# Seven block products in place of eight for the first expert of the first block

## The chip, the cores and the metric

The kernel runs on one core of a Trainium2 chip, in one launch. The metric is the time of one execution in microseconds. Its engines are TensorE (PE in the profile; its weight loads PEld), VectorE (DVE), ScalarE (ACT), GpSimd (POOL) and SyncE (SP), which issues nearly all transfers. All arithmetic is fp32.

## The reference

Two stages follow each other. A state-space layer (mamba2_ssd) works on 4 sequences of 768 tokens, 8 heads of 32 channels and a state of 16; its result is laid out as 3072 tokens of 256 features. On that works a mixture of four experts with all experts active:

```python
# per head, with the decays' running sums inside each chunk
y = (C B^T * L) x + (C state) * decay          # L: products of decays, causal
# then, x: (3072, 256), w1: (4, 256, 1024), w2: (4, 1024, 256)
p = domain_probs / (domain_probs.sum(-1, keepdims=True) + 1e-09)
for e in range(E):
    h = np.maximum(x @ w1[e], 0.0)
    out += p[:, e:e + 1] * (h @ w2[e])
```

## The kernel before

**Tiles.** The 3072 tokens are 24 chunks of 128. Two chunks make a *pair* of 256 tokens. Five *blocks* of pairs follow each other: three of two pairs (scheme B in the code) and two of three pairs (scheme H). The 1024 hidden features of an expert are four *feature blocks* `fb` of 256, sixteen over the four experts; expert 0 has 0 to 3, expert 1 has 4 to 7. A *block product* multiplies a 256x256 weight block's half with 256 tokens: two matmuls of 128x256 into one PSUM bank (`product`, L864).

**Fewer products.** Two feature blocks and two pairs of tokens make a 2x2 by 2x2 product of blocks, for which scheme B takes seven products where plain multiplication takes eight. This needs sums of weight blocks (`operands`, L955; stored in DRAM once made, L960, and loaded by later blocks, L952), sums of token blocks (`token_sums`, L974) and sums of the results. Scheme H does the same with three by three. Products are numbered in the code: in the first layer of scheme B, products 1 and 2 need only the first pair of tokens and the plain weights of the first feature block of the two; 6, 7, 5 and 3 need sums of weights, and 6, 7, 5 and 4 sums of tokens.

**The first layer with seven (`twos_first`).** Products accumulate in one bank, and intermediate values of the bank are kept aside: `snap` (L873) copies a bank to SBUF on ScalarE, `seed` (L878) copies such a value back into a bank, `combine` (L891) adds two of them on VectorE or GpSimd, and `gated` (L899) applies ReLU and the expert's gate on VectorE, out of the bank. The order for two feature blocks is 1, snap, 6, snap, 2 on a seed, 7, snap, 4, gate, 5 on a seed, gate, 3, subtraction in the bank (L1026), gate.

**The second layer (`second`, `visit`).** The results go into accumulators of two products each (a *house*) that are taken up and put down: seeded into a bank, added to, copied out (L1124, L1127).

**The state-space stage.** For each chunk `decays` scans the running products of decays on VectorE (L489), `fade` makes a part of the output operand on GpSimd (L499), `mask` the C operand on ScalarE (L465); `scores` multiplies (L472) and masks by VectorE (L788); `outputs` (L505, with the state L810) gives the tokens of the chunk, copied to SBUF by ScalarE (L825). The first two chunks are done by hand in a preamble that ends at about 13.2 us; there ScalarE also issues the store of decays to DRAM `ac_d` (L590), SP the store of the gates `p_d` (L691).

**The first block before the change.** It begins while chunks 2 and 3 (its second pair) are not yet there. Expert 0 goes by `plain_first`: its four feature blocks times the first pair, two plain products each, eight products in all, of which four stand ahead of `scores` of chunks 2 and 3 and four behind (SCORED). After `outputs` of chunks 2 and 3 come the second layer's terms 1 and 2 of expert 0, then eight plain products with the second pair, and only then experts 1 to 3 with seven products per two feature blocks.

**What sets the order.** TensorE's order (`line`) is written out by the code; `PAIRS_AT` says behind which product of which unit a later pair's scores and outputs stand. The order of all other engines is made at build time by `Plan`: it runs through the works with fixed costs (D512 and D256 for VectorE's 512- and 256-wide operations), gives each a latest time by the TensorE line, and lets each engine take the most urgent one that is ready. Works that both VectorE and GpSimd can do go to GpSimd if they are in time there and VectorE has a backlog (SLACK, BACK). The preamble is not in the plan: it starts at 13.2 us with fixed starting times. `NV` and `NW` are the numbers of value and weight tiles.

**DMA.** Eight completion semaphores, here called lanes, go round over all transfers in program order, SP's and ScalarE's together; a transfer is issued only when the one before it on its lane has landed.

Of the kernel before, what the change touches and what calls it, by code (L numbers as in the profile page):

```python
# [19 lines left out]
D512, D256 = .64, .36  # L20
LANDING = 2.2
KEEP = 5
NV, NW = 31, 28
SLACK, BACK, YIELD = 0.0, 3.0, 6.0
EARLY = 1, 2, 3, 4, 5, 6, 7, 8, 9, 10
# [4 lines left out]
HOLD = 12.0  # L30
NEAR, WORTH, FIRST = .3, 1.0, 25.0
# [3 lines left out]
SCORED = 4  # L35
# [39 lines left out]
class Plan:  # L75
# [105 lines left out]
    def run(self, line, at, begin):  # L181
# [19 lines left out]
        while todo:  # L201
# [4 lines left out]
            for w in waiting[e]:  # L206
# [5 lines left out]
                if len(w.on) > 1 and e == "POOL":  # L212
                    if max(ready, now) + w.on[e] > w.latest + late + SLACK or self.backlog(
                            waiting["DVE"], now, t["DVE"], w) < BACK:
                        continue
# [120 lines left out]
def kernel(  # L336
# [188 lines left out]
    a_sb = const.tile([NCH * NH // 2, 2, P], FP32, name="a_sb")  # L525
# [18 lines left out]
    for fb in range(2):  # L544
        load_w1(fb, homes["W"][fb])
# [39 lines left out]
    a_cut = const.tile([NCH * NH // 2, 2, P], FP32, name="a_cut")  # L585
# [8 lines left out]
    for fb in range(2, 4):  # L594
        load_w1(fb, homes["W"][fb])
    load_tokens(3, xb[3])
    for fb in range(2):
        load_w2(fb, homes["W"][4 + fb])
# [32 lines left out]
    gs = some(2, [P, NT, P], "gs")  # L631
# [93 lines left out]
    aq = plan.taken("V", NV - 2, 0.0)  # L725
    for c, i in ((2, 2), (3, 3)):
        st[c]["xb"] = plan.taken("xb", i, now)
# [192 lines left out]
    def operands(k, scheme, fbs, l, after=None, due=None, loaded=()):  # L920
# [3 lines left out]
        for f, fb in enumerate(fbs):  # L924
            v = loaded[f] if loaded else value("W")
            used = {x[1] for r, x in scheme.blocks[l].items() if x[0] == f and r != "b"}
            if loaded:
# [76 lines left out]
    def twos_first(k, fbs):  # L1004
# [8 lines left out]
        b1 = mul(1)  # L1013
        s1 = snap(b1)
        mul(6, b1)
        s6 = snap(b1)
        gate(0, 0, mul(2, seed(s1)))
# [83 lines left out]
    def visit(k, house, terms, last=False, only=None):  # L1101
# [20 lines left out]
        v.both = both  # L1122
# [144 lines left out]
    fbs = range(EPB)  # L1267
    for i in range(2):
        for l, j in ((1, i), (1, 2 + i), (2, i)):
            weights[0, j, l] = plan.taken("W", j + 4 * (l - 1), now + 1.0 + 0.6 * i)  # L1270
    for fb in (2, 3):
        v = weights[0, fb, 2] = value("W")
        dma(lambda e, fb=fb, v=v: load_w2(fb, v.t), part=[v])
# [4 lines left out]
    h, first = {}, {}  # L1278
# [9 lines left out]
    twos = [tuple(fbs[i:i + 2]) for i in range(0, EPB, 2)]  # L1288
    for two in twos:
        operands(0, B, two, 2, loaded=[weights[0, fb, 2] for fb in two])  # L1290
    line.extend(second(0, [(two, {1: h[two[0], 0], 2: h[two[1], 0]}) for two in twos], [(1, 2)]))
# [37 lines left out]
    for u, (k, groups) in enumerate(units):  # L1329
# [3 lines left out]
        if u + 1 < len(units):  # L1333
            unit_weights(*units[u + 1])
# [9 lines left out]
        else:  # L1344
            made = [(twos_first if b.scheme is B else threes_first)(k, fbs) for fbs in groups]
# [12 lines left out]
        else:  # L1358
            held = [(fbs, right(h)) for fbs, (_, h) in zip(groups, made)], b.scheme.houses
            plain_next = u + 1 < len(units) and units[u + 1][1] is None  # L1360
# [7 lines left out]
        if k < len(blocks) - 1:  # L1368
            for unit, x, what in PAIRS_AT[len(of_block), blocks[k + 1].scheme.pairs]:
# [72 lines left out]
```

## Time and profile before

| what | value |
|---|---|
| time, median of 3 runs | 624.41 us (624.24 to 624.74) |
| the profiled execution's own time | 624.57 us |
| its span in the profile | 622.6 us, so 1.97 us lie around it |
| TensorE busy | 616.9 us (99%) |
| VectorE, ScalarE, GpSimd busy | 532.1, 268.5, 171.6 us |
| DMA | 126.65 MB, 62.5% of 16 engines' span |
| granted TensorE clock | 0.998 |
| block matmuls with values of SBUF and with token sums | 436.6 + 203.3 us busy |

Busy time of an engine says how much of the span it worked; a matmul's records overlap, so TensorE's share counts stretches and the spacing of its instructions says what one costs. A fp32 matmul leaves two records. The profile's line numbers are those of the kernel printed above.

### The profile page before, as it was taken

How to read it: one execution, taken by the hardware profiler on the slowest of the kernel's cores; microseconds unless marked ns; L12 is line 12 of the kernel's file. 1: busy time of each engine (PE TensorE's matmuls, PEld its weight loads, DVE VectorE, ACT ScalarE, POOL GpSimd, SP SyncE). 2: the span in 40 equal slices, each digit the busy share in tenths (PEclk: the TensorE clock that was granted, in tenths of full speed). 3: DMA queues.
4: the chain of work that ended last, by engine and by line, in shares of the span. 5: the costliest groups of instructions: out<-in, count | busy, mean ns of one | idle time of the engine just before them, and what ended most of it. 6: DMA issues, size and time to landing. Idle time of an engine off the chain costs nothing.

```text
span 622.6 us, 10250 instructions
## 1 busy us (share of the span) xinstructions
PE 616.9 (99%) x3435; PEld 528.5 (85%) x3435; DVE 532.1 (85%) x883; ACT 268.5 (43%) x568; POOL 171.6 (28%) x199
## 2 busy tenths in 40 slices
PE   9999999999999999999999999999999999999997
PEld 5788888888888888888888888888888888888886
DVE  6999999997968799789689999959787987869684
ACT  4342464423356343236534336445443344555441
POOL 4536644740527754156350000100010000000010
PEclk9999999999999999999999999999999999999999
DMA  7999578673799978299999737535131424933001
GB/s 257 306 314 351 163 268 280 218 250 98 251 336 303 297 239 255 64 343 309 335 362 304 241 87 250 174 117 178 59 111 51 140 38 130 372 124 111 0 1 51
DMA packets 112307, 126.65 MB, mean 203 GB/s; under 512 B 28916, under 2 KB 78336, under 8 KB 112256
## 3 DMA queue, kind: packets, MB, share of 16 engines
q1 hardware_dynamic: 111988, 125.86, 62.5%
q8 instruction: 27, 0.44, 0.3%
q14 instruction: 24, 0.20, 0.1%
q10 hardware_dynamic: 268, 0.16, 0.1%
HBM read 101.09 MB, written 24.89 MB: 202 GB/s over the span
## 4 chain that ended last, share of the span: by engine, by line
PE 97%; DVE 1%; ACT 0%; issue 0%; DVEq 0%; ACTq 0%
PE bank L864 91%; PE bank L505 2%; PE bank L472 2%; DVE LT L489 1%; PE bank L644 1%; PE bank L810 1%; DVE MT L788 0%; PE bank L620 0%; PE bank L1245 0%; PE bank L612 0%; ACT A L515 0%; DVE v L899 0%; ACT v L687 0%; DVE v L1176 0%; ACT v L1250 0%
## 5 line engine op out<-in xcount | busy, mean ns | idle before, releaser
L864 PE MATMUL bank<-v,w 128*128 128x256 f32 x1856 | 436.6, 380 | 0.0
L864 PEld LDWEIGHTS bank<-v,w 128*128 128x128 f32 x1856 | 351.1, 190 | 51.9 <-issue 4.1
L891 DVE TENSOR_TENSOR v<-v,v 128x512 f32<-128x512 f32 x267 | 196.2, 764 | 16.0 <-ACT v L873 13.7
L864 PE MATMUL bank<-Y,w 128*128 128x256 f32 x792 | 203.3, 379 | 0.0
L864 PEld LDWEIGHTS bank<-Y,w 128*128 128x128 f32 x792 | 150.3, 190 | 20.9 <-issue 0.6
L899 DVE SCALAR_TENSOR_TENSOR v<-bank,gate 128x512 f32<-128x512 f32 x172 | 116.9, 684 | 34.5 <-PE bank L864 30.5
L878 ACT COPY bank<-v 128x512 f32<-128x512 f32 (+1 forms) x195 | 108.9, 570 | 62.8 <-DVE v L891 42.6
L955 POOL TENSOR_TENSOR w<-w,w 128x256 f32<-128x256 f32 x102 | 99.5, 997 | 53.8 <-PE bank L864 26.0
L873 ACT COPY v<-bank 128x512 f32<-128x512 f32 x106 | 62.1, 586 | 108.9 <-PE bank L864 108.7
L1124 ACT COPY v<-bank 128x512 f32<-128x512 f32 x105 | 61.5, 586 | 96.9 <-PE bank L864 96.4
L891 POOL TENSOR_TENSOR v<-v,v 128x512 f32<-128x512 f32 x11 | 15.6, 1414 | 247.9 <-DVE v L891 191.4
L489 DVE TENSOR_TENSOR_SCAN LT<-ab,ident 128x512 f32<-128x512 f32 x42 | 53.1, 1278 | 0.8 <-DMA ab<-acut_d 0.8
L891 DVE TENSOR_TENSOR v<-bank,v 128x512 f32<-128x512 f32 x40 | 27.6, 689 | 9.1 <-PE bank L864 8.9
L773 POOL TENSOR_TENSOR cts<-ctm,dec 128x256 f32<-128x256 f32 x20 | 18.2, 920 | 36.6 <-ACT ctm L465 24.3
L499 POOL TENSOR_TENSOR MT<-xb,LT 128x64 f32<-128x64 f32 (+1 forms) x28 | 16.2, 585 | 43.0 <-DVE LT L489 31.9
L788 DVE TENSOR_TENSOR MT<-bank,LT 128x512 f32<-128x512 f32 x44 | 27.2, 680 | 0.1
L1127 ACT COPY v<-bank 128x256 f32<-128x256 f32 x22 | 8.2, 373 | 38.0 <-PE bank L864 34.1
L1176 DVE TENSOR_TENSOR v<-v,v 128x256 f32<-128x256 f32 x52 | 20.3, 421 | 4.0 <-ACT v L1124 3.9
L465 ACT ACTIVATE ctm<-xb,tmask 128x128 f32<-128x128 f32 x48 | 16.4, 394 | 15.6 <-DMA xb<-in_xbc_dram 13.3
L1026 DVE TENSOR_TENSOR bank<-bank,v 128x512 f32<-128x512 f32 x22 | 15.2, 692 | 5.1 <-PE bank L864 5.0
L955 POOL TENSOR_TENSOR w<-w 128x256 f32<-128x256 f32 x14 | 13.7, 977 | 12.9 <-DMA w<-in_w_dram 7.8
L955 DVE TENSOR_TENSOR w<-w,w 128x256 f32<-128x256 f32 x36 | 15.4, 457 | 0.0
(71 smaller groups left out, 203.3 us busy)
## 6 DMA issues: line engine op xcount, KB each, us to landing
w<-w_d SPq DMA_DIRECT2D x134, 256.0 KB
w<-in_w_dram SPq DMA_DIRECT2D x128, 256.0 KB
w_d<-w SPq DMA_DIRECT2D x82, 256.0 KB
ab<-acut_d SPq DMA_DIRECT2D x21, 512.0 KB
w<-in_w_dram SPq DMA_DIRECT2D x40, 128.0 KB
gate<-p_d SPq DMA_DIRECT2D x10, 384.0 KB
xb<-in_xbc_dram SPq DMA_DIRECT2D x17, 192.0 KB
gate<-p_d SPq DMA_DIRECT2D x11, 256.0 KB
```

The costliest lines, as they stand in the source:

```text
L465: nc.scalar.mul(ctm[:, t], xb[:, OCT:OCT + P], tmask[:, t:t + 1])
L489: nc.vector.tensor_tensor_scan(out=LT.rearrange("p h s -> p (h s)")[:, lo:lo + w], data0=src, data1=ident.rearrange("p h s -> p (h s)")[:, ...
L773: plan.add({"POOL": .72}, lambda e: nc.gpsimd.tensor_mul(s["cts"].t, s["ctm"].t, s["dec"].t.unsqueeze(1).to_broadcast([HN, NT, P])), reads ...
L788: nc.vector.tensor_mul(s["MT"].t[:, js, h, 0:P], g, s["LT"].t[:, js, h])
L864: nc.tensor.matmul(out=o, lhsT=w[:, j], rhs=x if half is None else x[:, j], start=(start and j == 0), stop=(j == 1), skip_group_check=True)
L873: act(.5, lambda e: nc.scalar.copy(out=flat(v), in_=bank.t), reads=[bank], writes=[v])
L878: act(.54 if to - lo > FB else .32, lambda e: nc.scalar.copy(out=bank.t[:, lo:to], in_=flat(v)[:, lo:to]), reads=[v], writes=[bank])
L891: plan.add(engines, lambda e: (on(e).tensor_add if sign > 0 else on(e).tensor_sub)(flat(v), whole(x), whole(y)), reads=[x, y], writes=[v], ...
L899: dve(D512, lambda e: nc.vector.scalar_tensor_tensor(out=h.t, in0=whole(x).rearrange("p (j m) -> p j m", j=JJ), scalar=0.0, in1=g.t[:, 2 * ...
L955: plan.add({"POOL": .72} if due else B256, lambda e, r=r, x=x, y=y, sign=sign: (on(e).tensor_add if sign > 0 else on(e).tensor_sub)(view(r ...
L1124: act(.5, lambda e: nc.scalar.copy(out=flat(v), in_=bank.t), reads=[bank], writes=[v])
L1176: plan.add(engines, lambda e: (on(e).tensor_add if sign > 0 else on(e).tensor_sub)(o[1](), x[1](), y[1]()), reads=[v for v in vs if v is n ...
```

## The change

Expert 0 of the first block is computed with seven products too. `twos_begun` does products 1 and 2 of a pair of feature blocks (they need only the first pair of tokens), with a snap between them; it is done for four such pairs, those of experts 0 and 1, which are the eight products around `scores` of chunks 2 and 3 (now five ahead, three behind). `twos_first` then takes up a begun pair: it seeds the bank from the snap and goes on with product 6. After `outputs` of chunks 2 and 3 the second layer's term 1 of the four pairs follows (a house with one of its two halves; GpSimd clears the other), and then expert 0's remaining products. The initial loads change with it: w1 of the feature blocks 0, 2, 4, 6 and w2 of 0 and 2 first, the odd blocks later by the plan, and the gates of expert 1 early. Three tiles of the preamble (`a_sb`, `a_cut`, `gs`) move into value and weight tiles, which gives two more value tiles. The planner's constants change, and up to 40 us (EASY) GpSimd takes such shared works only at a backlog of 99 us.

Each function of the kernel after lies a few lines lower: L864 becomes L866, L873 L875, L878 L880, L899 L901, L955 L957, L1026 L1042.

```diff
-D512, D256 = .64, .36
+D512, D256 = .60, .34
-NV, NW = 31, 28
-SLACK, BACK, YIELD = 0.0, 3.0, 6.0
-EARLY = 1, 2, 3, 4, 5, 6, 7, 8, 9, 10
+NV, NW = 33, 28
+SLACK, BACK, YIELD = 0.0, 3.0, 0.0
+EARLY = 3, 4, 5, 5, 6, 7, 8, 9, 10, 11
-HOLD = 12.0
-NEAR, WORTH, FIRST = .3, 1.0, 25.0
+HOLD = 6.0
+NEAR, WORTH, FIRST = .3, 3.0, 25.0
-SCORED = 4
+SCORED = 5
+EASY = 40.0
 PAIRS_AT = {
-    (3, 2): ((0, 1, "s0"), (1, 5, "s1"), (1, 24, "o01")),
+    (0, 2): ((1, 12, "s0"), (2, 5, "s1"), (2, 22, "o01")),
...
-                            waiting["DVE"], now, t["DVE"], w) < BACK:
+                            waiting["DVE"], now, t["DVE"], w) < (BACK if now > EASY else 99):
...
-    for fb in range(2):
+    for fb in range(0, 4, 2):
         load_w1(fb, homes["W"][fb])
...
-    for fb in range(2, 4):
+    for fb in range(4, 8, 2):
         load_w1(fb, homes["W"][fb])
     load_tokens(3, xb[3])
-    for fb in range(2):
-        load_w2(fb, homes["W"][4 + fb])
+    for fb in range(0, 4, 2):
+        load_w2(fb, homes["W"][fb + 1])
     load_decays(3, homes["ab"][0])
...
+    def twos_begun(k, fbs):
+
+        seq = []
+        mul = opener(k, fbs, seq)
+        b1 = mul(1)
+        s1 = snap(b1)
+        mul(2, b1)
+        return seq, s1, gated(b1, gate_of(k, fbs[0]), 0)
+
-    def twos_first(k, fbs):
+    def twos_first(k, fbs, begun=None):
...
-        b1 = mul(1)
-        s1 = snap(b1)
+        if begun:
+            _, s1, h[0, 0] = begun
+            b1 = seed(s1)
+        else:
+            b1 = mul(1)
+            s1 = snap(b1)
         mul(6, b1)
         s6 = snap(b1)
-        gate(0, 0, mul(2, seed(s1)))
+        if not begun:
+            gate(0, 0, mul(2, seed(s1)))
...
-        v.both = both
+        v.both = both or len(house) == 2
+        if not both and len(house) == 2:
+            plan.add({"POOL": .4}, lambda e: nc.gpsimd.memset(
+                v.t[:, 1 - house.index(terms[0][0])], 0.0), part=[v])
...
+    twos = [(fb, fb + 1) for fb in range(0, 8, 2)]
...
-    for fb in fbs:
-        first[fb, 0], h[fb, 0] = plain_first(0, fb, 0)
+    for two in twos:
+        for l in (1, 2):
+            operands(0, B, two, l, loaded=loaded)
+    for i in range(2):
+        tokens[0, i + 1] = yT[0, 0], lambda v, i=i: v.t[:, i]
+    begun = {two: twos_begun(0, two) for two in twos}
+    firsts = [begun[twos[x + i]][0][j] for x in (0, 2) for j in range(2) for i in range(2)]
     decays(2)
     decays(3)
-    begun = [x for fb in fbs for x in first[fb, 0]]
-    line.extend(begun[:SCORED])
+    line.extend(firsts[:SCORED])
     scores([2, 3])
-    line.extend(begun[SCORED:])
+    line.extend(firsts[SCORED:])
     outputs([2, 3])
...
-    line.extend(second(0, [(two, {1: h[two[0], 0], 2: h[two[1], 0]}) for two in twos], [(1, 2)]))
+    line.extend(second(0, [(two, {1: h}) for two, (_, _, h) in begun.items()], [(1, 2)]))
...
-            if b.scheme is B and (k or g):
+            if b.scheme is B:
                 units.append((k, [(4 * g + i, 4 * g + i + 1) for i in (0, 2)]))
...
-    unit_weights(*units[0])
-    for fb in fbs:
-        first[fb, 1], h[fb, 1] = plain_first(0, fb, 1)
-    line.extend(x for fb in fbs for x in first[fb, 1])
     token_sums(0)
-    right = [(two, {r: v for r, v in twos_right({
-        (f, n): h[fb, n] for f, fb in enumerate(two) for n in range(2)}).items() if r > 2}) for two in twos]
-    behind = second(0, right, B.houses)
+    behind = []
```

More of the change, by code (lines that the diff above doesn't have):

```diff
@@ L524 @@
     pc = const.tile([P, NCH, E], FP32)
-    a_sb = const.tile([NCH * NH // 2, 2, P], FP32, name="a_sb")
+    a_sb, a_cut = (homes["V"][-4][:NCH * NH // 2, i].rearrange("p (r s) -> p r s", r=2) for i in range(2))
     nc.gpsimd.memset(aq0, 0.0)
@@ L584 @@
     clip(nc.gpsimd, a_sb)
-    a_cut = const.tile([NCH * NH // 2, 2, P], FP32, name="a_cut")
     nc.gpsimd.tensor_copy(a_cut, a_sb)
@@ L630 @@
     ctm = homes["ctm"]
-    gs = some(2, [P, NT, P], "gs")
+    gs = [homes["W"][-1][:, NT * P * i:NT * P * (i + 1)].rearrange("p (t s) -> p t s", t=NT) for i in range(2)]
     def aside(c, q, bank):
@@ L725 @@
     aq = plan.taken("V", NV - 2, 0.0)
+    plan.homes["V"][NV - 4].free = now + 3.0
+    plan.homes["W"][NW - 1].free = now
     for c, i in ((2, 2), (3, 3)):
@@ L918, in source, with operands @@
         return w2[e, f * FB:f * FB + FB, i * P:i * P + P].rearrange("(j p) m -> p j m", p=P)
-    def operands(k, scheme, fbs, l, after=None, due=None, loaded=()):
+    def operands(k, scheme, fbs, l, after=None, due=None, loaded={}):
         load, half = ((load_w1, w1_half), (load_w2, w2_half))[l - 1]
@@ L924, in operands @@
         for f, fb in enumerate(fbs):
-            v = loaded[f] if loaded else value("W")
+            v = loaded.get((fb, l)) or value("W")
             used = {x[1] for r, x in scheme.blocks[l].items() if x[0] == f and r != "b"}
-            if loaded:
+            if (fb, l) in loaded:
                 pass
@@ L1264, in put @@
         return [seqs[j][i] for _, j, i in sorted(keys)]
[L1267 to L1273, printed above, removed]
+    loaded = {}
+    for l, at in ((1, 0), (2, 1)):
+        for i, fb in enumerate(range(0, 8 // l, 2)):
+            loaded[fb, l] = plan.taken("W", fb + at, now + 1.0 + 0.6 * i)
+    twos = [(fb, fb + 1) for fb in range(0, 8, 2)]
     st[2]["a"] = [value("bank", fills=False) for _ in range(NQ)]
@@ L1277 @@
     pe(.72, lambda e: spread(2, [b.t for b in st[2]["a"]]), reads=[aq], writes=st[2]["a"])
-    h, first = {}, {}
-    for fb in fbs:
-        first[fb, 0], h[fb, 0] = plain_first(0, fb, 0)
+    for two in twos:
[5 more added lines that the diff above has]
+    firsts = [begun[twos[x + i]][0][j] for x in (0, 2) for j in range(2) for i in range(2)]
     decays(2)
     decays(3)
-    begun = [x for fb in fbs for x in first[fb, 0]]
-    line.extend(begun[:SCORED])
+    line.extend(firsts[:SCORED])
     scores([2, 3])
-    line.extend(begun[SCORED:])
+    line.extend(firsts[SCORED:])
     outputs([2, 3])
-    twos = [tuple(fbs[i:i + 2]) for i in range(0, EPB, 2)]
-    for two in twos:
-        operands(0, B, two, 2, loaded=[weights[0, fb, 2] for fb in two])
-    line.extend(second(0, [(two, {1: h[two[0], 0], 2: h[two[1], 0]}) for two in twos], [(1, 2)]))
+    line.extend(second(0, [(two, {1: h}) for two, (_, _, h) in begun.items()], [(1, 2)]))
     for c in range(4):
@@ L1332 @@
         i = u - of_block[0]
-        if u + 1 < len(units):
+        if 1 < u + 1 < len(units):
             unit_weights(*units[u + 1])
@@ L1344 @@
         else:
-            made = [(twos_first if b.scheme is B else threes_first)(k, fbs) for fbs in groups]
+            made = [threes_first(k, fbs) if b.scheme is H else twos_first(
+                k, fbs, begun.get(fbs) if k == 0 else None) for fbs in groups]
             seq = put(*[s for s, _ in made])
@@ L1359 @@
             held = [(fbs, right(h)) for fbs, (_, h) in zip(groups, made)], b.scheme.houses
+            for fbs, T in held[0]:
+                if k == 0 and fbs in begun:
+                    del T[1]
             plain_next = u + 1 < len(units) and units[u + 1][1] is None
@@ L1368 @@
         if k < len(blocks) - 1:
-            for unit, x, what in PAIRS_AT[len(of_block), blocks[k + 1].scheme.pairs]:
+            for unit, x, what in PAIRS_AT[len(of_block) if k else 0, blocks[k + 1].scheme.pairs]:
                 if unit != i:
```

## The prediction

> **What bounds the kernel now.** I read the page's busy row and chain first, then busy time by stretch, then the timeline of the opening, engine by engine. In the three rows by stretch the columns are the stretch and its length, then busy time (and instructions) of TensorE, weight loads, VectorE, ScalarE and GpSimd, the granted clock, the DMA share and GB/s.
>
> ```profile
> PE 616.9 (99%) x3435; PEld 528.5 (85%) x3435; DVE 532.1 (85%) x883; ACT 268.5 (43%) x568; POOL 171.6 (28%) x199
> ...
> PE 97%; DVE 1%; ACT 0%; issue 0%; DVEq 0%; ACTq 0%
> ```
>
> ```profile
> 13.20:23.30 10.10, 9.96 (x84) 7.63 (x80) 9.49 (x15) 3.49 (x12) 4.69 (x5) 1.00 0.99 315
> 23.30:36.00 12.70, 12.70 (x72) 10.72 (x70) 12.27 (x24) 3.08 (x13) 6.98 (x4) 1.00 1.04 344
> 36.00:618.00 582.00, 581.92 (x3199) 503.90 (x3199) 501.30 (x819) 255.66 (x527) 152.41 (x168) 1.00 0.61 199
> ```
>
> One piece of the chain in order of time (start, length, what, records) gives the spacing:
>
> ```profile
> 413.59 199.63 PE bank L864 x924
> ```
>
> TensorE sets the end: from 36 us to 618 us it idles 0.08 us of 582. So a matmul taken out there shortens the run by its own spacing, and any new wait lengthens it by its whole length. Two rows say where new waits are likely. In both early stretches VectorE is nearly full too (9.49 of 10.10, then 12.27 of 12.70 us), against 501 of 582 us later. The early timeline shows the one place where the chain leaves TensorE:
>
> ```profile
> 13.21 3.72 PE L864 MATMUL bank<-v,w 128*128 128x256 f32 x16
> 13.70 0.70 ACT L465 ACTIVATE ctm<-xb,tmask 128x128 f32<-128x128 f32 x2
> 13.84 2.39 DVE L489 TENSOR_TENSOR_SCAN LT<-bank,ident 128x256 f32<-128x256 f32 x4
> 14.79 0.52 SPq L430 DMA_DIRECT2D xb<-in_xbc_dram  x1
> 16.02 0.35 ACTq L590 DMA_DIRECT2D ac_d<-a_sb  x1
> 16.21 3.74 SPq L447 DMA_DIRECT2D w<-in_w_dram  x4
> 16.48 0.69 ACT L465 ACTIVATE ctm<-xb,tmask 128x128 f32<-128x128 f32 x2 [2.08 <-DMA ab<-acut_d]
> ...
> 19.65 2.48 DVE L788 TENSOR_TENSOR MT<-bank,LT 128x512 f32<-128x512 f32 x4
> 21.69 1.69 PE L505 MATMUL bank<-MT,xb 128*32 128x144 f32 x32
> 23.30 0.92 PE L864 MATMUL bank<-v,w 128*128 128x256 f32 x3
> ```
>
> The reader is to see three things: TensorE begins the block products at 13.21; ScalarE stands still from 14.40 until 16.02 in front of a DMA issue (the store of ac_d), and its mask of chunk 3 only follows at 16.48; the outputs of chunks 2 and 3 (L505) end at 23.30.
>
> **What it removes.** A product is two matmuls and leaves four records; 924 records in 199.63 us make 0.864 us each. Expert 0's first layer went as 16 plain products for its two pairs of feature blocks; seven each make 14. The second layer keeps seven terms per pair, and the built program has four block matmuls fewer. That is **-1.73 us**, all of it on the path.
>
> **What it adds.** Some 12 ScalarE copies (row mean 0.59 us), two subtractions into a bank and a few sums on VectorE, four more 256 KB loads of stored sums. After the opening ScalarE is idle for over half of the time and the queues for over a third: taken at 0. The constants reorder the whole run. Below nothing is excluded there (0.08 us idle in 582). Above, the nearest row is a bank's seed waiting for a gate ("ACT bank L878 <- DVE v L899", 18.4 us in 15 waits, 1.2 us each): one that loses its cover costs 1.2. I take 0, the row with the least idle time.
>
> **The opening, first stall.** The first eight products are now products 1 and 2 of four pairs of feature blocks. Product 2 accumulates into product 1's bank, and between them ScalarE must copy the bank out (the snap, L873). Before, no copy stood between the first eight. In the new program the first two snaps stand on ScalarE behind the ac_d store and behind the mask of chunk 3. That store waits for the DMA eight places ahead of it on its completion lane. Before, this was the 512 KB load of decays, issued at 10.59; now it is the second w2 load, issued one place earlier. The load that reuses this w2 load's lane is the row at 14.79, so the w2 load had landed by then. So: mask of chunk 2 ends 14.40; store 14.75 to 15.10; mask of chunk 3 15.2 to 15.9; snap 15.9 to 16.45. TensorE has finished its two first products by 13.21 + 1.73 = 14.94 and waits **1.5 us**. Ends: 0.1 us if store and mask were out of the way by 14.4; 2.9 us if the store still goes at 16.02.
>
> Then by spacing: three products to 19.05, scores (1.07) to 20.1, three products to 22.7. VectorE must gate the first bank before its scans: third product complete 17.5, gate (0.60) to 18.1, two scans of 1.13 to 20.35, second gate to 20.95, four masks (2.4) to 23.4. So the outputs begin in earnest at 23.45 and end at **24.57 against 23.30: +1.27 us**. Part of the 1.5 us falls into time that TensorE spent waiting for the masks anyway. At the ends of the stall this is 0 (scans and masks then stand as before) and 2.7 us.
>
> A rule bears on the store. The Trainium skill, DMA: Bandwidth & Descriptors, section "Anatomy of one DMA", gives about 2 us fixed and bytes over 436 GB/s (fitted on the GpSimd path). By it the w2 load issued at 8.80 lands at 11.4, an estimate, the stall is 1.15 us, and the whole sum below would be 0.35 us less. The row behind it: the 48 KB store of p_d went out at 11.03 to 11.88, and the load that waits for its lane stands at 16.21, so a transfer here took about twice the fixed price because the queue is full (DMA share 0.99).
>
> **SP's queue.** The gates of expert 1 (gate from p_d) now come second after that p_d store and must wait for it: SP is held from 12.4 to 16.2 us. Behind it stand the w1 of block 3, the w2 of blocks 1 and 3 and expert 1's odd blocks. The first then goes out at about 17.0, and VectorE first reads it at 25: eight microseconds of cover, against six between two uses of one lane in the rows (16.21 to 22.21). Taken at 0; without cover, up to 1 us.
>
> **The opening, second stall.** Before, the outputs were followed by four second-layer products and eight plain ones that need no sums; GpSimd took five of the weight sums between 16.7 and 31.8 us. Now only four second-layer products stand between, and no weight sum is on GpSimd before the fade of chunk 4; all are on VectorE. From 23.4 us until expert 0's gate of product 4 ends it has 25 sums of 128x256 (21 of weights, 4 of tokens), two gates, one 512-wide combine, then that gate. Thirteen sums start between 23.85 and 28.33 in the rows: 0.345 us, and 0.335 undisturbed. 25 x 0.335 + 4 x 0.60 = 10.8 us: the gate ends at 34.2, the seed of the same bank (0.59) at 34.9. TensorE needs from 24.57 ten products (8.64) to 33.2, and 0.45 more where three snaps stand behind the masks of chunks 4 and 5 on ScalarE: 33.7. It waits 1.25. The sister bank's seed then ends at 36.1 instead of 35.8 (0.33), and product 3 waits for a gate behind a scan of 1.13: 37.55 instead of 37.0 (0.55). Together **0.45 + 1.25 + 0.33 + 0.55 = 2.6 us**. The second-layer products of expert 0 that follow read gates and combines which, by the same spacings, end 3 to 6 us ahead of them: no further wait. Ends: 1.2 us, if the snaps cost nothing and some six sums less precede the gates; 3.6 us at the mean of 0.457 us that the page's group of these sums has (it holds those that met GpSimd).
>
> **Sum.** -1.73 + 1.27 + 2.6 = **+2.1 us**. The profiled execution took 624.57 us (span 622.6, 1.97 around it) and would take 626.7; it stands 0.16 above the median of 624.41, which becomes **626.5 us**, the span about 624.7.
>
> A second rule speaks about the gain. The Trainium skill, Perfetto Trace Analysis, section "Identifying the Most-Contended Engine", holds that matmul busy time is no measure of nearness to the limit and weight-load busy time is; that is 85% here. By it the removed products could be worth 85% of 1.73, an estimate of 1.47 us, and the sum +2.4. The row decides: products of one stretch follow each other every 0.864 us with no idle time.
>
> **Rivals.**
> *The cover holds, faster.* If the snap ends before 14.94 and the gate of product 4 before 33.0, only the removal is left: 622.7. For it: TensorE waits for nothing in 582 us of a program written out by the same planner, and the new costs, 0.60 and 0.34, are the rows' spacings. Against: the ac_d store and the wait for p_d are not in its plan, and the count of sums in front of the gate is fixed in the order. 0.16.
> *Half of it, same.* VectorE catches up (the low end, 1.2), and the first stall hides behind the masks but for 0.3: -1.73 + 0.3 + 1.2 = -0.2, 624.2; with one of the two as worked out, up to 625.2. 0.10.
> *More waits, slower still.* As forecast, and the new order loses its cover once (627.7) or twice (628.9) after 40 us, at 1.2 us each, or SP's hold shows (627.5). 0.10.
> *The change does not do what it says:* the four matmuls are gone in the built program; no chance given.
> *As worked out:* half of the way to each end, 625.2 (-1.73 + 0.65 + 1.9) to 627.8 (-1.73 + 2.0 + 3.1). 0.64, of which 0.04 below 625.7.
>
> **How the numbers follow.** What a measurement here can tell from no change is 0.2%, or 1.25 us: below 623.2 is faster, above 625.7 slower. Faster 0.16, same 0.10 + 0.04 = 0.14, slower 0.60 + 0.10 = 0.70. The range leaves out the rival below (0.16) and the far end above (about 0.04): 623.5 to 628.5.
>
> **What would show each step.** Block matmul records fewer by eight. The ac_d store at about 14.8 and the first snap ending near 16.4; TensorE idle some 1.5 us before its third product; outputs ending near 24.6. No weight sum on GpSimd before 36 us. Idle time of TensorE between 30 and 38 us, released by ScalarE seeds that wait for gates. From 40 us none. The prediction is wrong if TensorE is busy throughout 13 to 40 us, if the first snap comes by 15 us, or if the new waits stand after 40 us.

## The result, and the profile after

The changed kernel takes 628.51 us (median of seven runs, 627.22 to 629.82; an eighth, at a granted clock of 0.656, took 923.7 us and is left out) against 624.64 us for the kernel before, run beside it. The ratio is 1.0058 with a 95% interval of 1.0041 to 1.0076: slower by 2.6 to 4.7 us, 3.6 in the middle. The profiled execution took 629.19 us, its span 627.2 us, so 2.0 lie around it as before.

TensorE has eight block matmul records fewer (2640, not 2648), and each stretch has lost time. The busy row of the page after, then the busy time by stretch (columns as in the prediction):

```profile
PE 617.3 (98%) x3427; PEld 525.9 (84%) x3427; DVE 529.6 (84%) x886; ACT 274.6 (44%) x580; POOL 163.3 (26%) x201
```

```profile
12.68:24.75 12.07, 10.27 (x84) 7.50 (x81) 9.60 (x17) 5.31 (x14) 0.83 (x2) 1.00 0.80 271
24.75:38.00 13.25, 12.08 (x53) 8.93 (x51) 13.25 (x32) 8.82 (x26) 0.00 (x0) 1.00 0.96 341
38.00:618.00 580.00, 578.06 (x3183) 499.13 (x3182) 495.37 (x804) 253.50 (x522) 154.83 (x176) 1.00 0.62 200
```

TensorE is idle 1.8 us in the first row, 1.2 in the second, while VectorE is busy in all 13.25 of 13.25 us and GpSimd in none; and 1.9 us in the third, where it was 0.08 before. Who ended TensorE's waits (us in total, how many, the longest):

```profile
PE bank L866 <- ACT v L875: 3.0, 2, 1.7
PE bank L866 <- ACT bank L880: 0.9, 1, 0.9
...
PE bank L866 <- DVE MT L790: 0.7, 2, 0.3
```

Snaps (L875) ended 3.0 us in two waits, a seed (L880) 0.9 us, masks (L790) 0.7 us. The first snap wait is that of the opening, whose timeline answers to the one before:

```profile
12.68 1.99 PE L866 MATMUL bank<-v,w 128*128 128x256 f32 x8
13.16 0.69 ACT L466 ACTIVATE ctm<-xb,tmask 128x128 f32<-128x128 f32 x2
...
14.76 0.35 ACTq L590 DMA_DIRECT2D ac_d<-v  x1
15.21 0.69 ACT L466 ACTIVATE ctm<-xb,tmask 128x128 f32<-128x128 f32 x2 [1.36 <-DMA w<-in_w_dram]
15.81 1.05 ACT L875 COPY v<-bank 128x512 f32<-128x512 f32 x2
...
16.42 2.86 PE L866 MATMUL bank<-v,w 128*128 128x256 f32 x12 [1.75 <-ACT v L875]
...
23.15 1.67 PE L506 MATMUL bank<-MT,xb 128*32 128x144 f32 x32
```

ScalarE, done with the mask of chunk 2 at 13.85, stands until 14.76 in front of the store of ac_d, which a load of w releases; mask and snaps follow, and TensorE begins its third product at 16.42.

The second stall, as forecast, is a seed on ScalarE that waits for the gate of product 4 at the end of VectorE's queue:

```profile
33.68 0.69 DVE L901 SCALAR_TENSOR_TENSOR v<-bank,gate 128x512 f32<-128x512 f32 x1
...
34.45 0.59 ACT L880 COPY bank<-v 128x512 f32<-128x512 f32 x1 [1.52 <-DVE v L901]
...
35.10 2.33 PE L866 MATMUL bank<-Y,w 128*128 128x256 f32 x8 [0.86 <-ACT bank L880]
```

The other snap wait stands where nothing was expected, at 309 us:

```profile
309.22 0.69 ACT L466 ACTIVATE ctm<-xb,tmask 128x128 f32<-128x128 f32 x2 [2.79 <-DMA xb<-in_xbc_dram]
309.82 0.56 ACT L875 COPY v<-bank 128x512 f32<-128x512 f32 x1
...
310.43 0.92 PE L866 MATMUL bank<-Y,w 128*128 128x256 f32 x3 [1.28 <-ACT v L875]
```

A mask on ScalarE waits 2.79 us for a load of xb, and a snap that TensorE needs stands behind it. The two mask waits, at 378 and 406 us, have one pattern:

```profile
375.49 2.36 DVE L893 TENSOR_TENSOR v<-v,v 128x512 f32<-128x512 f32 x2
...
375.65 1.65 POOL L893 TENSOR_TENSOR v<-v,v 128x512 f32<-128x512 f32 x1 [28.57 <-DVE v L901]
...
377.77 1.87 DVE L790 TENSOR_TENSOR MT<-bank,LT 128x512 f32<-128x512 f32 x3
```

Two combines on VectorE take 2.36 us; without GpSimd they take 1.28 (e5 below). Here GpSimd runs one of its own beside them, and the masks come late.

For the account, take the spacing of neighbouring records of block products less the usual 0.216 us, summed by stretch where this excess is over 0.06; the right half of the table gives these sums in us, by stretches of time. Most first spacings behind a wait are 0.320 us, so that such a restart costs 0.104 us more; the kernel before has 1.98 us of restarts, behind scores and outputs. The runs were made in groups, each beside its own runs of the kernel before (medians 624.51 to 625.03), so kernels of different groups (e1 to e4, e5 to e8, e9 to e11, e12) are best compared by their ratios.

| kernel | median us | ratio to before, 95% | profiled run | 13-22 | 22-40 | 40-280 | 280-350 | 350-450 |
|---|---|---|---|---|---|---|---|---|
| before | 624.64 | | 624.57 | 0.21 | 0.21 | 0.94 | 0.31 | 0.31 |
| after | 628.51 | 1.0041-1.0076 | 629.19 | 2.22 | 2.74 | 1.04 | 2.06 | 1.51 |
| e1 | 626.78 | 1.0022-1.0051 | 626.60 | 0.84 | 2.66 | 1.04 | 0.41 | 1.50 |
| e2 | 628.63 | 1.0051-1.0079 | 629.11 | 1.72 | 2.49 | 2.23 | 0.31 | 1.51 |
| e3 | 629.24 | 1.0063-1.0093 | 630.79 | 1.27 | 2.74 | 3.06 | 1.39 | 1.51 |
| e4 | 627.69 | 1.0036-1.0064 | 628.32 | 0.84 | 2.41 | 2.22 | 0.31 | 1.50 |
| e5 | 626.73 | 1.0019-1.0045 | 629.03 | 0.73 | 2.66 | 1.04 | 4.31 | 0.31 |
| e6 | 630.74 | 1.0084-1.0113 | 628.72 | 0.83 | 1.44 | 4.15 | 0.57 | 1.50 |
| e7 | 625.39 | 1.0009-1.0026 | 625.99 | 0.21 | 0.21 | 1.04 | 0.92 | 0.98 |
| e8 | 627.21 | 1.0027-1.0050 | 627.20 | 0.37 | 0.96 | 4.15 | 1.60 | 0.31 |
| e9 | 627.07 | 1.0025-1.0053 | 629.68 | 0.83 | 2.66 | 1.04 | 4.51 | 0.31 |
| e10 | 632.72 | 1.0112-1.0139 | 631.80 | 1.33 | 2.59 | 7.77 | 0.31 | 0.31 |
| e11 | 626.40 | 1.0016-1.0037 | 626.07 | 0.37 | 0.96 | 2.32 | 1.81 | 0.31 |
| e12 | 625.93 | 1.0004-1.0029 | 624.81 | 0.37 | 0.97 | 2.32 | 0.57 | 0.31 |

The stretches are of the profiled run alone. For after they exceed those of before by 2.01 + 2.53 + 0.10 + 1.75 + 1.20 = 7.6 us; less 1.73 for the two products that makes 5.9 us, and from the first block product to TensorE's last record the profiles differ by 610.57 - 604.80 = 5.8. The profiled run began its products 0.53 us earlier (12.68, not 13.21) and ended 0.65 us sooner behind TensorE's last record, so its span is 4.6 us longer.

### The profile page after: what moved, and what is told of

Same layout as the page of the kernel before. It is cut to its first block, busy times and chain, and to the rows that moved or that the text cites. A ratio compares the mean times of both kernels' runs of the same rounds, so it can differ in the third digit from the quotient of the medians.

```text
span 627.2 us, 10263 instructions
## 1 busy us (share of the span) xinstructions
PE 617.3 (98%) x3427; PEld 525.9 (84%) x3427; DVE 529.6 (84%) x886; ACT 274.6 (44%) x580; POOL 163.3 (26%) x201
## 4 chain that ended last, share of the span: by engine, by line
PE 83%; DVE 8%; DMA 3%; SPq 3%; issue 2%; ACT 1%; POOL 0%; ACTq 0%; DVEq 0%; POOLq 0%
PE bank L866 79%; DVE v L893 3%; SPq L1250 2%; DMA w<-in_w_dram 2%; DVE v L901 2%; PE bank L506 1%; PE bank L473 1%; DMA xb<-in_xbc_dram 1%; DVE w L957 1%; DVE MT L790 1%; DVE LT L490 1%; PE bank L812 1%; DVE v L1195 0%; ACT v L875 0%; ACT A L516 0%
## 5 line engine op out<-in xcount | busy, mean ns | idle before, releaser
L866 PE MATMUL bank<-v,w 128*128 128x256 f32 x1816 | 428.4, 380 | 2.0 <-ACT v L875 1.7
L866 PEld LDWEIGHTS bank<-v,w 128*128 128x128 f32 x1816 | 343.1, 190 | 53.9 <-issue 2.8
L866 PE MATMUL bank<-Y,w 128*128 128x256 f32 x824 | 211.7, 380 | 2.9 <-ACT v L875 1.3
L893 DVE TENSOR_TENSOR v<-v,v 128x512 f32<-128x512 f32 x269 | 188.8, 735 | 26.1 <-ACT v L875 24.7
L866 PEld LDWEIGHTS bank<-Y,w 128*128 128x128 f32 x824 | 155.6, 190 | 27.5 <-ACT v L875 2.7
L880 ACT COPY bank<-v 128x512 f32<-128x512 f32 (+1 forms) x200 | 112.2, 571 | 81.1 <-DVE v L893 47.0
L901 DVE SCALAR_TENSOR_TENSOR v<-bank,gate 128x512 f32<-128x512 f32 x172 | 116.6, 683 | 31.6 <-PE bank L866 26.9
L875 ACT COPY v<-bank 128x512 f32<-128x512 f32 x112 | 65.3, 584 | 101.5 <-PE bank L866 101.2
L957 POOL TENSOR_TENSOR w<-w,w 128x256 f32<-128x256 f32 x105 | 91.6, 894 | 40.2 <-PE bank L866 18.4
L1143 ACT COPY v<-bank 128x512 f32<-128x512 f32 x105 | 61.4, 584 | 90.4 <-PE bank L866 88.0
L893 POOL TENSOR_TENSOR v<-v,v 128x512 f32<-128x512 f32 x11 | 18.4, 1669 | 281.4 <-DVE v L893 142.6
L790 DVE TENSOR_TENSOR MT<-bank,LT 128x512 f32<-128x512 f32 x44 | 27.3, 680 | 1.2 <-PE bank L473 1.2
L957 POOL TENSOR_TENSOR w<-w 128x256 f32<-128x256 f32 x14 | 16.1, 1155 | 37.4 <-DMA w<-in_w_dram 18.9
L775 POOL TENSOR_TENSOR cts<-ctm,dec 128x256 f32<-128x256 f32 x20 | 16.2, 816 | 26.7 <-ACT ctm L466 19.7
L1042 DVE TENSOR_TENSOR bank<-bank,v 128x512 f32<-128x512 f32 x24 | 16.4, 687 | 3.5 <-PE bank L866 3.5
L957 DVE TENSOR_TENSOR w<-w,w 128x256 f32<-128x256 f32 x33 | 15.4, 503 | 0.0
```

Source lines behind the costliest of these rows:

```text
L790: nc.vector.tensor_mul(s["MT"].t[:, js, h, 0:P], g, s["LT"].t[:, js, h])
L866: nc.tensor.matmul(out=o, lhsT=w[:, j], rhs=x if half is None else x[:, j], start=(start and j == 0), stop=(j == 1), skip_group_check=True)
L875: act(.5, lambda e: nc.scalar.copy(out=flat(v), in_=bank.t), reads=[bank], writes=[v])
L880: act(.54 if to - lo > FB else .32, lambda e: nc.scalar.copy(out=bank.t[:, lo:to], in_=flat(v)[:, lo:to]), reads=[v], writes=[bank])
L893: plan.add(engines, lambda e: (on(e).tensor_add if sign > 0 else on(e).tensor_sub)(flat(v), whole(x), whole(y)), reads=[x, y], writes=[v], ...
L901: dve(D512, lambda e: nc.vector.scalar_tensor_tensor(out=h.t, in0=whole(x).rearrange("p (j m) -> p j m", j=JJ), scalar=0.0, in1=g.t[:, 2 * ...
```

## The experiments

**e1 to e4: one cause at a time.** Each is one line of the changed kernel:

```diff
-    store_decays(nc.scalar, ac_d, a_sb)     # e1, e4
+    store_decays(nc.sync, ac_d, a_sb)
-EASY = 40.0                                 # e2, e4
+EASY = 0.0
-SLACK, BACK, YIELD = 0.0, 3.0, 0.0          # e3, e4
+SLACK, BACK, YIELD = 0.0, 3.0, 6.0
```

Expected of e1:

> The changed kernel, but the store of ac_d is issued by SyncE (nc.sync) and no longer by ScalarE. Theory: the first stall (TensorE without work from 14.3 to 16.4 us, 2.0 us in the trace of after) exists because ScalarE stands in front of this store until 14.76 and only then masks chunk 3 and takes the first snap. With the store gone from ScalarE the mask of chunk 3 ends about 1 us earlier, the snap with it: a first stall of 0.7 to 1.1 us in place of 2.0, outputs of chunks 2 and 3 ending 0.7 to 1.2 us before 24.75, and the time 0.7 to 1.2 us below after; the gaps between 33 and 38 us move with it but keep their length. Rival: VectorE sets the opening (gates, scans, masks in a row, busy 9.5 of 10.1 us). Then the snap comes earlier but the outputs still end at 24.6 to 24.8, and the time stays within 0.3 us of after. Second rival: SyncE, which now has to wait for the store's lane, sends the next loads later, and the time rises by up to 1 us.

Measured: 626.78 us, and the timeline of SyncE's queue, ScalarE and TensorE:

```profile
12.07 0.50 SPq L590 DMA_DIRECT2D ac_d<-v  x1
...
13.69 1.28 ACT L466 ACTIVATE ctm<-xb,tmask 128x128 f32<-128x128 f32 x4
...
15.48 2.86 PE L866 MATMUL bank<-v,w 128*128 128x256 f32 x12 [0.28 <-ACT v L875]
```

The masks run through, the third product begins at 15.48, the outputs end at 23.80 (0.95 earlier, as expected), and the gaps behind keep their length (1.02, 0.23 and 0.41 us, all 0.95 earlier). The first stall falls from 1.91 us (spacing above the usual) to 0.45, further than expected, since products began at 13.21 here and at 12.68 in after. So ScalarE's wait in front of the store made most of the first stall; with the mask of chunk 3 behind the snaps (e8 below) the rest goes too. SyncE did not wait at all: the store went out at 12.07, straight behind that of p_d, and the trace puts it on another lane, last used at 6.41. A store on ScalarE with a free lane was not tried. The medians differ by 1.7 us, more than expected; the profiled run of e1 also met no late load at 309 us.

Expected of e2:

> The changed kernel with EASY = 0 in place of 40: the planner may give weight sums of the first 40 us to GpSimd again. Theory: the stalls between 33.8 and 38 us (1.0 + 0.23 + 0.41 us and 0.1 more for each in the trace of after) come from VectorE having all 25 sums ahead of the gate of product 4. With some of them on GpSimd VectorE reaches that gate sooner: these stalls shrink from about 2.0 us to 0.5 to 1.2, and the time falls by 0.8 to 1.5 us. Rival: sums on GpSimd slow VectorE's own two-input work by the port that they share (0.457 us against 0.335 for a sum in the rows of before), so that the gate ends no sooner: time within 0.4 us of after, the stalls still about 2 us. A second rival: the queue of VectorE is not what the gate waits for (a load of weights is late); then nothing changes either, and the gate's releaser in the trace is a DMA.

Measured: 628.63 us; no gain. Five sums went to GpSimd from 29.9 us on, and the combine in front of the gate of product 4 slowed from 0.69 to 1.07 us:

```profile
32.24 1.07 DVE L893 TENSOR_TENSOR v<-v,v 128x512 f32<-128x512 f32 x1
```

The next combine took 1.21 us. The gaps are 0.76 and 0.76 us in place of 1.03, 0.23 and 0.41, and a new one of 1.0 us stands at 111 us, behind a sum on GpSimd. The first rival was right: the gate of product 4 begins 0.25 us earlier (33.43, not 33.68), so most of what VectorE hands over it loses again beside GpSimd.

Expected of e3:

> The changed kernel with YIELD = 6 as before, not 0: on VectorE a combine of two inputs stands back again when the planner has GpSimd on the shared port. Theory: the two stalls that nobody expected at 378 and 406 us (0.59 us each with the restart) come from this constant: there GpSimd takes a combine while VectorE runs two of its own, which take 2.36 us for two in place of 1.28, and the masks behind them are late. With YIELD = 6 both stalls vanish, and the time falls by 1.0 to 1.3 us; the opening (both early stalls) is unchanged to 0.1 us. Rival: these stalls come from the new order of the whole run (other constants, two more V buffers, the seven-product scheme in expert 0) and not from YIELD: the same stalls stay or stand elsewhere after 40 us with a total within 0.5 us of 3.0, and the time is within 0.4 us of after.

Measured: 629.24 us. The stalls at 378 and 406 us are unchanged (0.50 and 0.49), and others came at 91, 116, 340 and 348 us. The theory that YIELD makes them fell.

Expected of e4:

> The changed kernel with all three edits: store of ac_d on SyncE, EASY = 0, YIELD = 6. Theory (the waits are separate and add up): 0.7 to 1.2, 0.8 to 1.5 and 1.0 to 1.3 us are saved together, 2.5 to 4.0 us below after, which is 624.6 to 626.1, about the time of before or up to 1.5 us above it. Rival: the waits do not add, because VectorE's row of work in the opening takes back what each edit gives (each saves alone, together they save no more than the larger one): 1.0 to 1.6 us below after, 627.0 to 627.6.

Measured: 627.69 us, above e1 alone and just above the rival's 627.0 to 627.6. What adds is the store; the other two edits add nothing or cost.

**e5 to e9: the finished order changed by hand.** To move a step without a new plan, e5 and all later ones but e7 and e10 start from e1 and edit the order that the planner has made, by the works' numbers:

```diff
+    def behind_of(m, *ns, by=None):      # emit works ns right behind work m
...
+    def swap_banks(n, m):                # the bank that n seeds <-> the one that m seeds, from there on
...
+    behind_of(1890, 1729, by="DVE"); behind_of(2015, 1833, by="DVE")       # e5, e8, e9, e11, e12
+    swap_banks(192, 115); swap_banks(206, 129)                             # e6, e8, e11, e12
+    behind_of(111, 115); behind_of(125, 129); behind_of(128, 192, 206)     # with the swap
+    behind_of(131, 112, 126, 251)        # combines and a scan behind the gates: e6, e8, e11, e12
+    behind_of(64, 82); behind_of(206, 263, 254)                            # masks: e8, e11, e12
+    behind_of(1295, 1635, 1636)                                            # scans: e9, e11
+    behind_of(1436, 1638, 1640, 1647); behind_of(1361, 1883, 1885, 1875, 1877)   # masks: e9, e11, e12
     for w in done:
         w.fn(w.by)
```

Expected of e5:

> The kernel of e1, and in its finished order two combines (L893, 128x512) are taken from GpSimd, given to VectorE and put behind the four masks that follow; everything else keeps its engine and its place. Theory: the stalls at 376 and 404 us of e1 (0.49 + 0.10 us each) come from these combines: while GpSimd runs one (1.64 us), VectorE's own two take 2.35 us together in place of 1.28, and the masks behind them release TensorE's banks late. With them moved the masks start about 1.1 us earlier, both stalls vanish, and the time falls by 1.0 to 1.3 us against e1 (626.78), to 625.5 to 625.8. Rival: the two combines of VectorE are slow by themselves or the masks wait for something else (the scores' end, a load): the stalls stay within 0.1 us of 0.49 and the time within 0.4 us of e1. A third way: the combines, now later on VectorE, are missed further on and a new stall of up to 1 us appears within 15 us behind.

Measured: with the combines away from GpSimd VectorE's two take 1.28 us, and both stalls are gone (0.31 us between 350 and 450, as in before):

```profile
376.94 1.28 DVE L893 TENSOR_TENSOR v<-v,v 128x512 f32<-128x512 f32 x2
```

That shows their cause. The third way did not come: no new stall stands behind. The time of the theory was missed all the same, the median did not move (626.73): the seven runs spread from 625.47 to 629.03, and the profiled one, the slowest, has 4.3 us of stalls between 280 and 350 us, where loads are late. VectorE waits 4.50 us for ab at 284.57 with gates behind the waiting scan.

Expected of e6:

> The kernel of e1 with two changes of its finished order between 25 and 38 us. (a) PSUM banks: the two seeds of expert 1's pairs, which stand ready at 25.6 and 26.6 us for products at 40 us, take the banks that the gates of product 4 release; the seeds of product 5 take the two banks that are free. (b) On VectorE two combines and a scan of 1.23 us stand behind the gates of product 5, not between the gates. Theory: the second stall is the queue of VectorE ahead of the gates together with the banks that wait for these gates. Then the seeds of product 5 (L880) follow their snaps at once, the gaps of 1.02 and 0.23 us go, that of 0.41 falls below 0.4, and the time is 1.2 to 1.9 us below e1 (626.78): 624.9 to 625.6. Rival: VectorE is simply full (12.00 of 12.00 us busy), so that work put back is missed at once: the same total of stalls, 1.5 to 2.0 us, stands between 34 and 48 us, and the time is within 0.4 us of e1.

Measured: 630.74 us. The gaps of the second stall went (1.44 us between 22 and 40, from 2.66), but 3.1 us came back between 54 and 69 us. Time and place are not the rival's (within 0.4 us of e1, stalls between 34 and 48 us). Nor is VectorE full ahead of the gates of product 4 any more: it waits 0.35 and 0.44 us for their products. What came back later has the pattern of e8 below: at 44.93 us two scans take 3.37 us beside a combine of GpSimd. Banks and order were changed together, so the part of each in the second stall is not known. The other three runs lie 2 us above the profiled one; what they have in addition no trace shows.

e7 is the kernel before with five of the change's constants (EARLY, among others, stays as before):

```diff
-D512, D256 = .64, .36
+D512, D256 = .60, .34
-SLACK, BACK, YIELD = 0.0, 3.0, 6.0
+SLACK, BACK, YIELD = 0.0, 3.0, 0.0
-HOLD = 12.0
-NEAR, WORTH, FIRST = .3, 1.0, 25.0
+HOLD = 6.0
+NEAR, WORTH, FIRST = .3, 3.0, 25.0
```

> The kernel before with only the planner's constants of the change that can be taken alone: costs .60 and .34, YIELD 0, HOLD 6, WORTH 3. First layer of expert 0 stays at 16 plain products, the opening stays. Theory: the late stalls (376 and 404 us in e1, 0.59 each with the restart) come from the planner's new constants, since they order the whole run; then this kernel has 0.5 to 1.5 us of stalls after 60 us and takes 625.0 to 626.0, with its opening as in before. Rival: they come from the change of structure, which shifts every later step against the loads and the other engines; then this kernel has none after 60 us, and its time is within 0.5 us of before (624.4).

Measured: 625.39 us, the whole interval above 1. The constants alone cost 0.5 to 1.6 us, with stalls of 0.26 us at 343 and 0.56 at 403 us, late as the theory had it, though not at the places of e1's. They come in part from the constants, then; which of the five is open. The loads of xb that before issues at 281 us go out at 288.6.

Expected of e8:

> The kernel of e1 with the moves of e5 and e6, and two more in its finished order: ScalarE's mask of chunk 3 stands behind the first two snaps, and the masks of chunks 4 and 5 behind the seeds of product 5. Theory: each stall had its own cause, so the four moves add: 0.5 us at 15 us, 1.2 to 1.9 us between 28 and 38 us and 0.3 to 0.6 us at the snaps there, 1.0 to 1.3 us at 376 and 404 us. Together 3.0 to 4.2 us below e1 (626.78): 622.6 to 623.8, which is under before (624.4). TensorE then waits less than 1.5 us in all between 13 and 40 us. Rival: VectorE takes back what the opening gains, as it is full until 48 us: 1.5 to 2.4 us below e1, 624.4 to 625.3, no faster than before.

Measured: 627.21 us, above both expectations. The opening is nearly clean (0.37 and 0.96 us to 40 us), yet four stalls came between 54 and 69 us. VectorE and GpSimd in e1, then in e8, around 44 us:

```profile
44.05 2.34 DVE L490 TENSOR_TENSOR_SCAN LT<-ab,ident 128x512 f32<-128x512 f32 x2
46.30 1.87 DVE L893 TENSOR_TENSOR v<-v,v 128x512 f32<-128x512 f32 x3
47.19 2.11 POOL L893 TENSOR_TENSOR v<-v,v 128x512 f32<-128x512 f32 x1 [6.91 <-ACT v L875]
```

```profile
44.06 3.37 DVE L490 TENSOR_TENSOR_SCAN LT<-ab,ident 128x512 f32<-128x512 f32 x2
44.70 1.64 POOL L893 TENSOR_TENSOR v<-v,v 128x512 f32<-128x512 f32 x1 [4.41 <-ACT v L875]
...
47.34 3.41 DVE L893 TENSOR_TENSOR v<-v,v 128x512 f32<-128x512 f32 x3
```

VectorE is at the same scan at the same time. A snap that comes earlier lets GpSimd begin its combine at 44.70, not 47.19, and VectorE's same five steps take 6.8 us in place of 4.2. The opening's gain made another engine start sooner, and by e11 below this cost 1.83 of the 2.17 us that the opening had gained over e1.

Expected of e9:

> The kernel of e5, and in its finished order the steps around 285 to 310 us that wait for a late load stand further back on their engines: the two scans of one chunk on VectorE (due at 317 us, they stood at 281) 12 us later, four masks on ScalarE (two due at 314 us, two at 368 us, they stood at 295 to 306) 5 to 14 us later, with the fades of ctm on GpSimd that follow three of them. Theory: the stalls of 3.5 us at 290 to 312 us in the profiled run of e5, like that at 309 us in after, arise because these steps stand in an in-order queue in front of gates, seeds and snaps and wait there for xb and ab, which land late in some executions; that is also why e5's runs spread from 625.47 to 629.03. With the steps further back no stall stands between 280 and 320 us, the median falls from 626.73 to 625.3 to 625.8, and the spread of the runs below 1.2 us. Rival: the loads themselves are late for everything (weights too), so the stalls come back at another step: median within 0.4 us of e5, spread as before.

Measured: 627.07 us, 625.89 to 629.68. In the profiled run 4.5 us of stalls stand at 300 to 315 us, now with scans of 1.74 us each on VectorE and a snap behind seeds that wait for late gates. The rival was right: moving the waiting steps does not help here.

**e10: the structure with the old constants.** The counterpart of e7:

```diff
-D512, D256 = .60, .34
+D512, D256 = .64, .36
-SLACK, BACK, YIELD = 0.0, 3.0, 0.0
-EARLY = 3, 4, 5, 5, 6, 7, 8, 9, 10, 11
+SLACK, BACK, YIELD = 0.0, 3.0, 6.0
+EARLY = 2, 3, 4, 5, 6, 7, 8, 9, 10, 11
-HOLD = 6.0
-NEAR, WORTH, FIRST = .3, 3.0, 25.0
+HOLD = 12.0
+NEAR, WORTH, FIRST = .3, 1.0, 25.0
-EASY = 40.0
+EASY = 0.0
```

> The changed kernel's structure with the planner's constants of before: .64 and .36, YIELD 6, HOLD 12, WORTH 1, the early sums spread one by one over units 2 to 11, EASY 0 (the same numbers of buffers, and SCORED 5, as in after). The counterpart to e7. Theory: the opening's stalls come with the structure and stay (2.0 us at 16 us, 1.5 to 2.5 us between 28 and 40 us); the loads of xb at 282 us go out as early as in before, and nothing waits for them at 290 to 312 us; the stalls at 378 and 406 us are gone, since these costs order the combines otherwise. Time 626.3 to 627.5. Rival: under the old costs the planner misjudges the fuller opening and loses its cover between 40 and 90 us as well, by 2 us or more: 628 to 631. Then the new constants were needed for this structure, and their late stalls are their price.

Measured: 632.72 us, above both expectations. The opening's stalls are there (1.33 and 2.59), those at 378 and 406 us are not, but one wait of 4.92 us stands at 73.8 us, where masks stand behind four scans on VectorE. The xb loads go out at 289.5 us, so the old constants do not bring them back. With e7: the new constants cost 0.5 to 1.6 us by themselves and, set against all the old ones together, spare this structure some 4 (ratio 1.0126 against 1.0058). Behind that wait some 1.7 us more go to a lower clock (last section).

**e11 and e12: what the rest is made of.**

```diff
+    behind_of(261, 262)                  # e11, e12: GpSimd's fade ahead of its combine
+    behind_of(390, 219)                  # e12: a gate behind a mask
+    behind_of(1141, 1634); behind_of(1151, 1632); behind_of(1315, 1641)    # e12: loads of ab, xb earlier
```

Expected of e11:

> The kernel of e8 with the moves of e9, and one step of GpSimd moved: the fade that waits for the scans of chunks 4 and 5 (L500, L769 in the code) stands ahead of GpSimd's first combine, so that this combine (L893, 128x512) can no longer begin while VectorE scans. Theory: e8's four stalls between 54 and 69 us (0.97, 0.23, 0.46, 0.88 us, each with 0.1 for the restart) come from the port: at 44.05 us VectorE is at the same scan in e1 and in e8, but in e8 GpSimd begins its combine at 44.7 in place of 47.2, VectorE's two scans take 3.37 in place of 2.34 us and the three combines 3.41 in place of 1.87, and the gate behind them comes at 50.7, not 48.3. With GpSimd held until the scans end, VectorE reaches that gate by 48.9, these four stalls vanish (2.9 us), and so does that at 310 us (1.3 us): 622.8 to 624.2, under before (624.6). Rival: VectorE is too full for the work that the opening put back, whatever GpSimd does: two or more of the four stalls stay, at least 1.2 us of them, and the time is 624.8 to 626.5.

Measured: 626.40 us. The scans take 2.34 us again, the gate comes at 49.65 (48.9 was expected, since the combines still meet GpSimd), and of the four stalls 0.97 and 0.46 us are gone, 0.22 and 0.88 stay. So the time is the rival's, and the causes are mixed: GpSimd's early start made more than half of the four stalls (1.83 of 3.11 us); that a full VectorE makes the rest was not tried by itself.

Expected of e12:

> The kernel of e11, with the two scans of the chunk due at 317 us back in their place at 281 us and, instead, the loads that are waited for there moved up in SyncE's order: the first ab load by some ten loads (4 us), the two xb loads by six and seven (5 to 8 us); the four masks of ScalarE stay further back as in e9. One more step: the gate at 65.7 us (L901) stands behind the second of the four masks around it, not the first. Theory: what is left above before in e11 is the stall at 299.6 us (0.90), at 308.6 (0.29) and at 66.4 (0.88), each with 0.1 for the restart. With the loads early the first two vanish (1.4 us), with the gate behind a mask the third falls to 0.3 or 0.4 (0.5 us): 624.3 to 625.0, level with before (624.6 to 625.0). Rival: the loads moved up push other loads back (the queues' share is 0.8 to 1.0 there), so that the stalls between 285 and 315 us stay at 1 us or more in sum, and the gate put back makes the stall behind it longer: 626.0 to 627.0, no better than e11.

Measured: 625.93 us, 624.52 to 626.43, ratio 1.0004 to 1.0029, between the two expectations. The stalls at 299.6 and 308.6 us are gone (0.57 us between 280 and 350); the gate's place made no difference, 0.88 us stay at 66.4. This is the best version, and it does not beat the kernel before: of the 3.6 us (from the ratio 1.0058) it takes back 2.6. Its profiled run, 624.81 us, is the second fastest of twelve; what the median run has on top of it no trace shows.

## Why the prediction was right, and where it was wrong

The direction and the opening's mechanism were right. The point, 626.5, was 2.0 us too low, and the median of 628.51 stands at the very end of the range: the kernel lost 3.6 us by the ratio where 2.1 were forecast. By the prediction's own signs, waits after 40 us would show it wrong, and they came: 3.05 of the 7.6 us of new waits in the profiled run.

- **Removal, -1.73.** Eight records fewer, spacing 0.216 us as before. The account closes within 0.1 us with 1.73 (5.9 against 5.8); with the prediction's other estimate, 1.47, it would miss by 0.35.
- **First stall, +1.27.** The store at 14.76 (14.8 forecast), snaps from 15.81, third product at 16.42 (16.45), outputs ending at 24.75 (24.57). e1 shows the named cause. The wait was 1.9 us and not 1.5, because this run's first product began at 12.68; e2 and e3 have the same order on ScalarE, began at 13.2, and waited 1.41 and 0.95 us. The size depends on when the store's lane comes free (the store went out at 14.35 to 14.78 in these three, not at the 11.4 of the prediction's second estimate; that a full queue makes transfers last so long is argued there, and no run varies it). From the first block product to the end of the outputs the opening takes 12.07 us for 10.10, 2.0 more; on the clock of the run the 0.53 us of the earlier start hide part of it.
- **SP's queue, 0.** The gate load went out at 16.51 (16.2), and nothing waited for what stood behind it.
- **Second stall, +2.6.** Measured 2.53. No weight sum was on GpSimd before 38 us, the seed of product 5 waited for the gate of product 4, and the gaps were 1.03, 0.23 and 0.41 us with 0.1 each for the restart, and about 0.6 at the snaps behind masks. The queue of VectorE stood there as forecast, and the banks that wait for its gates belong to it (e6); what e2, e6 and e8 add is that none of the ways tried relieved it at no cost. In e1 VectorE is busy in 24.00 of the 24 us from 24 to 48 us, and in 39.85 of 40 from 60 to 100, and most of what was taken from the opening came back later as contention or as a wait.
- **"The constants reorder the whole run ... I take 0": the step that failed.** The term was put at the low end of its own range. The row that it took (0.08 us idle in 582) belonged to the old order and says nothing of a new one. In the profiled run 3.05 us stand behind 40 us: 1.20 at 378 and 406 us, the same in the profiles of after and of e1 to e4 and e6 (e5: GpSimd's combines beside VectorE's), and 1.75 between 280 and 350 us, where the profiled runs of these kernels differ (none of it in e2, 4.0 in e5; e12: loads that go out late). The loads of xb go out at 281 us in before, at 291 in after, and at 288.6 with the new constants alone (e7). The rival "more waits" came close in size, two of 1.2 us at a chance of 0.10, but not in kind: it had seeds that wait for gates, and what came were masks late behind contended combines and steps that wait for loads.
- **"The queues for over a third: taken at 0".** An average again: the DMA share in after, 0.62 from 38 us on, is 1.00 from 270 to 290 us and 0.94 from 290 to 310. There some steps wait for loads, and moving loads ahead (e12) removed the stalls.
- **A slip in the rival "half of it".** With the second stall as worked out and the first at 0.3 its sum is -1.73 + 0.3 + 2.6 = +1.2, which is 625.6, not 625.2; both lie below the 625.7 above which the prediction counted slower, so its chances stand.

Against the Trainium skill: SBUF — State Buffer, section "SBUF: two separate sides", says that a VectorE instruction with two SBUF inputs and a GpSimd instruction that reads SBUF lock one shared port for the whole instruction, and that the loser waits fully. The rows come near: two combines of 1.28 us and one that takes GpSimd 1.27 us elsewhere (at 39.80 us in before) would be 2.55 us one after the other, and took 2.36. The prediction did not apply this to the new order's later part.

## What to carry to other kernels

When an edit makes a planner write the whole program anew, the waits after the edited stage are a term of the sum with its own price, and the idle time of the old order is no bound for it. On a full engine, look for what a step that comes earlier will set free: here (e8) GpSimd, released 2.5 us sooner, worked beside VectorE's scans, and five steps of VectorE took 2.6 us longer. A store that waits for its lane on a compute engine's queue stands in front of all that follows there, 0.9 us on ScalarE here; moving it to SyncE, where it did not wait, was the one edit among e1 to e3 that gained.

## What was not expected of the hardware

A long wait of TensorE cost more than its length in two runs. In e9 a spacing of 2.31 us between two records was followed by spacings of 0.427 us in place of 0.216 for 3.0 us, and the granted clock fell; columns as above:

```profile
308.40:310.60 2.20, 0.33 (x2) 0.00 (x0) 1.07 (x2) 1.47 (x4) 1.99 (x4) 1.00 1.01 364
310.60:314.40 3.80, 3.74 (x10) 3.06 (x11) 2.32 (x4) 2.19 (x5) 0.00 (x0) 0.59 1.05 374
```

In e10 the same followed the spacing of 5.14 us (clock 0.57). By the excess spacings that is some 1.7 us on top in both. Behind the spacing of 2.12 us in after there is none. The Trainium skill, TensorE: Matmul & The Clock Gate, section "Why this matters for your kernels", advises against idle gaps over about 3 us; here a spacing of 2.31 us was already too long, and the measurement decides.

What stays open: why the first block product begins at 12.6 to 13.2 us in different runs, and why the loads between 270 and 310 us land so differently between the profiled runs.
